# Attention with memory and a gated feed-forward: diagonal score blocks packed at 64 tokens, 18 score visits a segment in place of 20

## Chip, cores and metric

One core of one Trainium2 chip runs the whole program in one launch. The metric is the device time in microseconds. TensorE is called PE, its weight loader PEld, VectorE DVE, ScalarE ACT, GpSimd POOL, and SyncE, which issues nearly all transfers, SP.

## The reference

The input x has 2048 tokens of 640 features. After a layer norm (xn) there are two branches, and the result is `x + s * g`.

- s: attention with 32 heads of 20 features. The tokens are cut into 4 segments of 512. In a segment each head attends causally to the tokens of that segment alone, and also reads a memory made from all segments before.
- g: `silu(down(sigmoid(xn Wgate) * (xn Wup)))`, with 1536 inner features.

```python
logits = jnp.einsum('bhqd,bhkd->bhqk', qs, ks) * scale + mask     # mask: query < key
p = _softmax(logits, axis=-1)
a_dot = jnp.einsum('bhqk,bhkd->bhqd', p, vs)
pq = phi(qs)
num = jnp.einsum('bhld,bhde->bhle', pq, M)
den = jnp.einsum('bhld,bhd->bhl', pq, z)[..., None] + 1e-06
o = g * (num / den) + (1.0 - g) * a_dot
pk = phi(ks)
M = M + jnp.einsum('bhld,bhle->bhde', pk, vs)
z = z + jnp.einsum('bhld->bhd', pk)
```

All data are bfloat16.

## The kernel before

Heads are taken in 8 groups of four. In a group, head r lies in the row strip of 32 partitions from 32r (20 features of the head and 4 rows that carry a bound, 24 in all), so that four score products of four heads run side by side in four row strips of PE. `QT` and `KT` hold the transposed queries and keys of half of the groups; they come through DRAM (`stage_out`, `relay`, `c_out`, `c_in`).

Scores are made transposed: keys on partitions, queries on columns. A *visit* (`scores`, line 628) fills `Sps`, one tile of four PSUM banks, 512 columns for each of the four heads. One exponential on ACT (line 639) takes the whole tile to `pt` in SBUF, of which there are four buffers; `Sps` has one. The causal mask is put on afterwards by POOL with affine selects (line 643), which set the upper part of the diagonal blocks to zero.

Of the 512 x 512 scores of a head, only blocks of 128 keys by the queries from the block on are made: 4 x 128 columns on the diagonal and 768 beside it, 1280 in all. Two groups (a pair) make 2560 columns, five visits of 512. `UNITS` is the table of these five: which group of the pair, which key block, which query blocks, how many, and at which column. Units 0 and 3 hold the four diagonal blocks of a group and are masked with four selects each. A segment has 4 pairs, 20 visits (`NSLOT`), the kernel 80.

`weigh_group` (line 661) multiplies the exponentials of one group by the values: `AT` is 128 x 512, head r on partitions 32r to 32r+31 (column strips of PE), the weights are V with a column of ones beside each head (`VW` = 21), so that row 20 of a strip is the softmax denominator. ACT copies AT to `ats` scaled by the gate's share, an SP transpose makes `Asb`, `divide` on DVE divides, `o_add` adds the memory's part `om`.

All other products are full size: v, k and q of the next segment, gate, up and down, the output product, the memory reads (`am`). The same function `mm` (line 193) can issue each of them as four column strips of 32 output partitions (line 196) in place of one (line 199); it does so in the slots just before an AT (`columns`).

Order: the engines' instructions are written out by hand. A slot is one visit. Python code at build time fills each slot: first AT if one is due, then the visit's scores, then *tasks* (products with a due time in slots, from `PLAN`) and *bulk* (gate, up, down) up to a common level. `PLAN` has due times in slots for every segment: `v`, `k`, `q` products, `pk`/`pq` (phi), `stats`/`norm`, `proj`, `read`, transfers `wd`, `wo`, `xr`, `rows`, and a correction of the bulk for each slot, `bias`. `LAG` has the delays after an AT, in slots. `later` puts something a while after its task. So the order on each engine is fixed; what waits at run time are semaphores.

SP issues transfers and transposes in its own fixed order. The startup (line 707) is written out separately; the main loop begins at the first scores (33.2 us in the profile); after the last AT (297.4 us) the last down products and the output product follow.

Of the kernel before, what the change touches and what calls it, by code (L numbers as in the profile page):

```python
# [9 lines left out]
P = 128  # L10
S = 2048
D = 640
# [41 lines left out]
NU = len(UNITS)  # L54
NSLOT = NG // 2 * NU
# [5 lines left out]
LAG = [0.5, 2.9, 1.9]  # L61
LAST = (NSEG - 1, NG // 2 - 1)
# [4 lines left out]
    dict(glu=[-1.9, -4.08],  # L67
         wd=[4.2, 7.1, 5.93, 5.73],
         wo=[18.5, 20.03],
         v=[1.4, 1.63, 2.65, 3.07, 3.82, 4.8, 5.74, 6.86],  # L70
         k=[5.3, 7.42, 7.86, 8.11, 8.64],
         q=[10.0, 10.58, 11.02, 13.03, 15.22],
         pk=[8.9, 9.37, 10.91, 12.19, 13.55],
         pq=[13.9, 14.48, 15.42, 16.05, 18.25],
         pk0=[0.41, 1.17, 2.49],
         bound=16.1,
         upd=[9.12],
         norm=[-1.9, -0.26],
         late=4.1,
         rows=[11.82, 12.73],  # L80
         bias=[-0.2, -0.3, 0.0, 0.1, 0.0, 0.4, -0.3, 0.5, 0.2, 0.0, 0.4, 0.1, -0.1, -0.1, -0.3, 0.2, 0.4, -0.2, 0.0, -0.3],
         dg=[0, 1, 0, 0]),
    dict(v=[2.8, 3.74, 4.2, 4.5, 4.79, 5.23, 5.54, 6.62],
         k=[6.1, 7.53, 7.69, 8.63, 10.59],
         q=[13.0, 13.26, 13.64, 14.61, 15.74],
         pk=[9.2, 9.5, 11.64, 13.19, 13.89],
         pq=[14.7, 15.49, 15.61, 16.18, 18.08],
         bound=17.0,
         upd=[9.16],
         stats=[-1.9, -1.23, -2.6, -1.59],  # L90
         norm=[-0.2, 0.84, 2.41, 2.85],
         proj=[6.4, 7.01, 7.37, 8.1, 9.14, 10.03, 11.29, 12.57],
         read=[2.2, 2.88, 3.42, 4.8, 5.37, 5.77, 6.53, 6.86],
         turn=[2.6, 2.72, 3.87, 4.97],
         xr=[3.93, 5.14, 5.18, 9.5],
         rows=[10.32, 10.94],
         bias=[-0.8, 0.7, -0.1, -0.1, 0.2, -0.2, -0.2, -0.5, -0.3, 0.0, 0.7, 0.3, 0.0, -0.1, -0.1, 0.1, -0.5, 0.1, -0.1, 0.0],
         dg=[0, 0, 0, 1]),
    dict(v=[2.5, 2.71, 4.39, 4.62, 5.59, 6.19, 6.59, 7.25],
         k=[7.6, 8.6, 8.82, 10.45, 10.63],  # L100
         q=[11.7, 11.92, 12.21, 12.71, 13.01],
         pq=[13.9, 14.67, 17.25, 17.4, 18.21],
         bound=14.3,
         upd=[10.97],
         stats=[-1.9, -0.84, 1.22, 2.68],
         norm=[-0.7, 0.06, 2.22, 4.3],
         proj=[4.7, 4.88, 5.44, 6.41, 8.53, 9.28, 9.51, 9.97],
         read=[2.9, 4.34, 4.71, 5.64, 6.52, 7.12, 7.61, 9.05],
         turn=[3.2, 3.91, 4.6, 5.28],
         xr=[2.53, 3.76, 4.58, 6.49],  # L110
         bias=[0.3, -0.1, 0.6, -1.1, -0.4, -0.5, 0.8, 0.2, 1.2, -0.4, 0.6, 1.3, -0.1, -0.4, -0.2, 0.3, 0.3, -0.3, -0.2, -0.1],
         dg=[0, 1, 1, 1]),
    dict(proj=[5.7, 6.98, 7.43, 8.44, 9.0, 10.74, 11.23, 11.81],
         read=[2.7, 3.67, 5.0, 5.2, 6.87, 7.73, 8.63, 9.25],
         turn=[3.6, 4.03, 5.33, 5.39],
         xr=[3.83, 4.67, 7.15, 9.08],
         xl=[-8.0, -5.88, -5.57, -5.21],
         bias=[0.1, 0.1, 0.1, 0.1, -0.4, 0.0, 0.0, 0.2, 0.1, -0.8, 0.1, 1.0, -0.3, 0.4, -0.5, 0.0, 0.5, 0.0, -0.3, -0.5],
         dg=[0, 1, 0, 1]),
# [4 lines left out]
def kernel(  # L124
# [130 lines left out]
    wt = cpool.tile([P, P], BF, name="wt")  # L255
    nc.vector.memset(wt[:], 0.0)
# [7 lines left out]
    for i in range(8):  # L264
        V.append(cpool.tile([P, H + 1, VW], BF, name=f"va{i}"))
    QT = [cpool.tile([P, 4, L], BF, name=f"QT{i}") for i in range(3)]
    KT = [cpool.tile([P, 4, L], BF, name=f"KT{i}") for i in range(3)]
    nInd = cpool.tile([P, DC, H], F32, name="nInd")
    BD = cpool.tile([P, DC, HW, VW], BF, name="BD")
# [14 lines left out]

    def make_ind():

        nc.gpsimd.memset(nInd[:], -1.0)
        nc.gpsimd.affine_select(out=nInd[:], in_=nInd[:], compare_op=ALU.is_ge, fill=0.0,
                                base=0, pattern=[[P, DC], [-DH, H]], channel_multiplier=1)
        nc.gpsimd.affine_select(out=nInd[:], in_=nInd[:], compare_op=ALU.is_ge, fill=0.0,  # L290
                                base=DH - 1, pattern=[[-P, DC], [DH, H]], channel_multiplier=-1)

    def make_bd(a, b):
        if a == 0:
            nc.gpsimd.memset(BD[:], 1.0)
# [14 lines left out]
    def gates():  # L310
        th = cpool.tile([P, H], F32, name="th")
        nc.scalar.activation(th[:], beta_b[:], ACT.Tanh, scale=0.5)
        gcol = cpool.tile([P, H], F32, name="gcol")
        gin["omg"] = cpool.tile([P, H], F32, name="omg")
        gin["ginv"] = cpool.tile([P, H], F32, name="ginv")
        nc.vector.tensor_scalar(gcol[:], th[:], 0.5, 0.5, op0=ALU.mult, op1=ALU.add)
        nc.vector.tensor_scalar(gin["omg"][:], th[:], -0.5, 0.5, op0=ALU.mult, op1=ALU.add)
        nc.vector.reciprocal(gin["ginv"][:], gcol[:])
# [148 lines left out]
    def v_tile(n, j, half):  # L467
# [6 lines left out]
        evacuate(va[:, half * 16:(half + 1) * 16, 0:DH], ps[:].rearrange("p (h e) -> p h e", e=DH))  # L474

# [19 lines left out]
    def m_update(n):  # L495
# [11 lines left out]
        dmb = stg.tile([P, DC, WIN, VW], BF, name="dmb", bufs=2)  # L507
# [120 lines left out]
    def scores(n, pair, u):  # L628
        half = pair // 2
        qt, kt = half_tile(QT, n, half), half_tile(KT, n, half)  # L630
        for (dg, kb, qb, cnt, c0) in UNITS[u]:
            gi = 2 * pair % 4 + dg
            for r in range(4):
                nc.tensor.matmul(Sps[:, r, c0:c0 + cnt * P],  # L634
                                 lhsT=kt[32 * r:32 * r + KR, gi, kb * P:(kb + 1) * P],
                                 rhs=qt[32 * r:32 * r + KR, gi, qb * P:(qb + cnt) * P],
                                 start=True, stop=True, tile_position=(32 * r, 0))
        pt = ptp.tile([P, 4, L], BF, name="pt")
        nc.scalar.activation(pt[:], Sps[:], ACT.Exp, scale=SCALE)  # L639
        if u in (0, 3):  # L640
            for r in range(4):
                diag = pt[:, r, :].rearrange("p (x c) -> p x c", c=P)
                nc.gpsimd.affine_select(out=diag, in_=diag, compare_op=ALU.is_ge, fill=0.0, base=0,  # L643
                                        pattern=[[0, 4], [1, P]], channel_multiplier=-1)
        return pt

    def parts(dg):
        return [(u, kb, qb, cnt, c0) for u in range(NU) for (d, kb, qb, cnt, c0) in UNITS[u] if d == dg]

# [11 lines left out]
    def weigh_group(now, n, pair, dg, pts):  # L661
        g = 2 * pair + dg
        AT = dtile([P, L], F32, "AT")
        mine = sorted(parts(dg), key=lambda m: m[0] == 3 + PLAN[n]["dg"][pair])
        for i, (u, kb, qb, cnt, c0) in enumerate(mine):
            v = V[4 * (n % 2) + kb][:].rearrange("p h e -> p (h e)")
            for r in range(4):
# [168 lines left out]
    for n in range(NSEG):  # L836
# [46 lines left out]
        for slot in range(NSLOT):  # L883
# [7 lines left out]
            elif u == 3:  # L891
                weigh_group(now, n, pair, 0, pts)
# [60 lines left out]
```

## Time and profile before

Three runs took 317.45, 319.76 and 320.02 us; the median is 319.76. The profiled execution took 317.42 us.

| | profile before |
|---|---|
| time of the profiled execution | 317.42 us |
| its span (first to last instruction) | 315.7 us |
| granted PE clock, mean | 0.999 |
| PE busy | 306.9 us (97%) |
| ACT busy | 250.5 us (79%) |
| DVE busy | 202.5 us (64%) |
| POOL busy | 133.9 us (42%) |
| exponentials (line 639) | 80, 1876 ns each |
| selects (line 643) | 128, 664 ns each |
| DMA engines | 52.4% of the span |

Busy time is the time in which an engine runs at least one instruction; the rest is idle time, and the profile names what ended it. Idle time of an engine that does not set the end costs nothing. A PE product takes some 0.2 us longer from start to end than its columns need, since products overlap; so PE's pace is read from the distance of starts, not from the duration of one.

### The profile page before, as it was taken

What the parts mean: (1) busy time and instruction counts of PE and PEld (TensorE: products, weight loads), DVE (VectorE), ACT (ScalarE), POOL (GpSimd) and SP (SyncE); (2) the same over time, 40 slices, a digit from 0 to 9 for tenths busy, and PEclk for the clock granted to TensorE, in tenths of its full rate; (3) what the DMA queues carried; (4) which work ended last, traced back from release to release, by engine and by line L of the source; (5) the groups of instructions that cost most, each with busy time, mean ns of one, the idle gap of its engine ahead of it and who ended that gap; (6) DMA issues with size and microseconds to landing.
All of it is one profiled execution on the core that took longest, in us unless ns stands there. A gap on an engine that the chain in (4) does not pass through costs nothing.

```text
span 315.7 us, 11686 instructions
## 1 busy us (share of the span) xinstructions
PE 306.9 (97%) x4989; PEld 175.7 (56%) x5021; DVE 202.5 (64%) x472; ACT 250.5 (79%) x284; POOL 133.9 (42%) x248
## 2 busy tenths in 40 slices
PE   7999999999999999999999999999999999999995
PEld 6544555545574566545566565645466655544773
DVE  6476653596885657688767867787554487733345
ACT  7654899999997886797888878887998978889530
POOL 4176424273355230483316543377444333643305
PEclk9999999999999999999999999999999999999999
DMA  7985995957965770645531494245400452330042
GB/s 235 356 267 160 233 175 159 274 151 184 158 137 106 86 139 23 193 99 156 128 104 36 92 129 117 83 142 171 98 20 21 77 126 62 102 77 19 19 69 83
DMA packets 71395, 39.95 MB, mean 127 GB/s; under 512 B 46000, under 2 KB 71344, under 8 KB 71344
## 3 DMA queue, kind: packets, MB, share of 16 engines
q1 hardware_dynamic: 71200, 39.05, 52.4%
q8 instruction: 39, 0.64, 0.9%
q10 hardware_dynamic: 144, 0.16, 0.1%
q14 instruction: 12, 0.10, 0.1%
HBM read 20.19 MB, written 8.39 MB: 91 GB/s over the span
## 4 chain that ended last, share of the span: by engine, by line
PE 96%; DVE 1%; issue 1%; DMA 1%; POOL 0%
PE gp L199 12%; PE up L199 12%; PE yp L199 10%; PE Sps L634 8%; PE yp L196 7%; PE psq L199 6%; PE AT L669 6%; PE psk L199 5%; PE up L196 5%; PE gp L196 5%; PE psv L199 5%; PE sp L199 5%; PE sp L196 2%; PE psv L196 2%; PE psk L196 2%; PE psq L196 1%
## 5 line engine op out<-in xcount | busy, mean ns | idle before, releaser
L639 ACT ACTIVATE pt<-Sps 128x2048 bf16<-128x2048 f32 x80 | 150.1, 1876 | 14.4 <-PE Sps L634 12.8
L643 POOL TENSOR_SCALAR_AFFINE_SELECT pt<-pt 128x512 bf16<-128x512 bf16 x128 | 80.5, 664 | 138.3 <-ACT pt L639 138.2
L554 DVE SCALAR_TENSOR_TENSOR hT<-hT,up 128x512 bf16<-128x512 bf16 x48 | 32.9, 685 | 38.4 <-ACT hT L543 17.8
L199 PE MATMUL gp<-xnT,Wg 128*128 128x512 bf16 x162 | 43.4, 380 | 0.8 <-issue 0.5
L199 PE MATMUL up<-xnT,Wu 128*128 128x512 bf16 x159 | 42.4, 379 | 1.4 <-issue 1.1
L543 ACT ACTIVATE hT<-gp 128x512 bf16<-128x512 f32 x48 | 28.6, 598 | 9.2 <-PE gp L199 8.8
L199 PE MATMUL yp<-Wd,hT 128*128 128x320 bf16 x230 | 34.1, 300 | 0.0
L634 PE MATMUL Sps<-QT,KT 24*128 24x128 bf16 (+2 forms) x896 | 31.9, 241 | 0.0
L573 DVE SCALAR_TENSOR_TENSOR aa<-t,yp 128x320 bf16<-128x320 bf16 x32 | 15.3, 480 | 24.9 <-ACT t L571 24.8
L673 ACT ACTIVATE ats<-AT,share 128x512 bf16<-128x512 f32 x32 | 22.0, 688 | 9.2 <-PE AT L669 8.5
L199 PEld LDWEIGHTS <-hT 128*128 128x128 bf16 x230 | 21.6, 98 | 10.3 <-issue 1.1
L199 PEld LDWEIGHTS <-Wu 128*128 128x128 bf16 x172 | 16.1, 98 | 17.8 <-issue 0.6
L199 PEld LDWEIGHTS <-Wg 128*128 128x128 bf16 x172 | 15.8, 98 | 17.8 <-issue 1.5
L634 PEld LDWEIGHTS <-KT 24*128 24x128 bf16 x896 | 13.1, 92 | 21.7 <-issue 20.5
L669 PE MATMUL AT<-pt,va 128*32 128x128 bf16 (+2 forms) x896 | 23.5, 242 | 0.1
L196 PE MATMUL yp<-Wd,hT 128*32 128x320 bf16 x616 | 22.6, 300 | 0.0
L571 ACT ACTIVATE t<-yp 128x320 bf16<-128x320 f32 x32 | 13.9, 438 | 9.2 <-PE yp L199 6.7
L669 PEld LDWEIGHTS <-va 128*32 128x32 bf16 x896 | 17.8, 97 | 5.8 <-DVE aa L611 0.3
L656 DVE TENSOR_TENSOR od<-Asb,rd 128x320 bf16<-128x320 bf16 x32 | 18.2, 568 | 2.6 <-DVE rd L655 1.6
L611 DVE SCALAR_TENSOR_TENSOR aa<-aa,sp 128x320 bf16<-128x320 bf16 x32 | 15.4, 483 | 6.7 <-PE sp L199 4.4
L199 PE MATMUL psq<-xnT,Wq 128*128 128x512 bf16 x81 | 19.3, 379 | 0.3 <-issue 0.2
L196 PEld LDWEIGHTS <-hT 128*32 128x32 bf16 x616 | 15.7, 97 | 5.5 <-issue 1.5
(97 smaller groups left out, 454.3 us busy)
## 6 DMA issues: line engine op xcount, KB each, us to landing
xt<-in_A_x_dram SPq DMA_DIRECT2D x8, 320.0 KB
KT<-Ks SPq DMA_DIRECT2D x32, 80.0 KB
QT<-Qs SPq DMA_DIRECT2D x32, 80.0 KB
Wg<-in_B_w_gate_dram SPq DMA_DIRECT2D x3, 640.0 KB
Wu<-in_B_w_up_dram SPq DMA_DIRECT2D x3, 640.0 KB
Wd<-in_B_w_down_dram SPq DMA_DIRECT2D x4, 480.0 KB
xr<-in_A_x_dram SPq DMA_DIRECT2D x12, 160.0 KB
out_dram<-xr SPq DMA_DIRECT2D x12, 160.0 KB
```

Source lines behind the costliest of these rows:

```text
L196: nc.tensor.matmul(ps[b:b + 32], lhsT=lhsT[:, b:b + 32], rhs=rhs, start=start, stop=stop, tile_position=(0, b), skip_group_check=True)
L199: nc.tensor.matmul(ps, lhsT=lhsT, rhs=rhs, start=start, stop=stop, skip_group_check=True)
L543: nc.scalar.activation(h[:], gp[:], ACT.Tanh, scale=0.5)
L554: empty(lambda: nc.vector.scalar_tensor_tensor(out=h[:], in0=h[:], scalar=1.0, in1=ps[:], op0=ALU.add, op1=ALU.mult), own)
L573: empty(lambda: nc.vector.scalar_tensor_tensor(out=aa[:, hs], in0=t2[:], scalar=1.0, in1=yp[:], op0=ALU.add, op1=ALU.mult), own)
L611: nc.vector.scalar_tensor_tensor(out=aa[:, hs], in0=aa[:, hs], scalar=0.25, in1=sp[:], op0=ALU.mult, op1=ALU.mult)
L634: nc.tensor.matmul(Sps[:, r, c0:c0 + cnt * P], lhsT=kt[32 * r:32 * r + KR, gi, kb * P:(kb + 1) * P], rhs=qt[32 * r:32 * r + KR, gi, qb * P ...
L639: nc.scalar.activation(pt[:], Sps[:], ACT.Exp, scale=SCALE)
L643: nc.gpsimd.affine_select(out=diag, in_=diag, compare_op=ALU.is_ge, fill=0.0, base=0, pattern=[[0, 4], [1, P]], channel_multiplier=-1)
L656: nc.vector.tensor_tensor(s["od"][:, :, 4 * g * DH:(4 * g + 4) * DH].rearrange("p q (r e) -> p q r e", e=DH), A[:, :, :, 0:DH], rd[:].unsq ...
L669: nc.tensor.matmul(AT[32 * r:32 * r + 32, qb * P:(qb + cnt) * P], lhsT=v[:, h0:h0 + 32], rhs=pts[u][:, r, c0:c0 + cnt * P], start=(i == 0) ...
L673: nc.scalar.activation(ats[:], AT[:], ACT.Identity, scale=gin["share"][:, g:g + 1])
```

## The change

Each 128 x 128 diagonal block is cut at 64. Its right part (the last 64 queries against all 128 keys) joins the columns beside it: kinds 0 to 3, `UPPER`, 448, 320, 192 and 64 columns. Its left part needs only the first 64 keys against the first 64 queries. Two of these small blocks, of two key blocks, are put into the same 64 columns, one on partitions 0 to 63, one on 64 to 127: kinds 4 and 5. A group then has 1024 + 128 = 1152 columns, four groups (a half) 4608, nine visits. `VISITS` is the table: group, kind, column, width. A segment has 18 visits, the kernel 72. Visits 0, 3, 5 and 7 of a half hold packed pieces, and in them every score product is issued with 64 keys as weights, two for each strip, on eight strips (32 rows by 64 columns); in the other visits with 128 keys as before.

For AT, a packed piece is multiplied twice, each time over all 128 partitions: with `VE`, whose lower half is zero, and with `VO`, whose upper half is zero. VE holds the first 64 tokens of V tiles 0 and 2, VO those of tiles 1 and 3, moved 64 partitions down; `v_low` copies them by four SP transfers a segment, `v_zeros` sets the zero halves once, on POOL in the startup.

Masks: in a packed piece two selects on 64 partitions each, in the first part of each kind 0 to 3 one over 64 columns; pieces that stand 256 columns apart are done together. It makes 240 selects for 128.

The AT of groups 0 to 3 of a half stand ahead of its slots 3, 5, 7 and 9 (the ninth is slot 0 of the next half); before, one stood at units 3 and 0 of each pair. All due times in `PLAN` and the delays `LAG` are new. W_down comes in 12 transfers of one tile (160 KB) in place of 4 of three. To make room in SBUF, `wt` and `BD` share a buffer with `om`, `nInd` is bfloat16, `dmb` has one buffer and the gate's small tiles are reused.

```diff
-UNITS = [
-    [(0, kb, kb, 1, kb * P) for kb in range(4)],
-    [(0, 0, 1, 3, 0), (0, 2, 3, 1, 384)],
-    [(0, 1, 2, 2, 0), (1, 1, 2, 2, 256)],
-    [(1, kb, kb, 1, kb * P) for kb in range(4)],
-    [(1, 0, 1, 3, 0), (1, 2, 3, 1, 384)],
+HP = P // 2
+UPPER = [(kb, kb * P + HP, L - kb * P - HP) for kb in range(4)]
+VISITS = [
+    [(0, 4, 0, 64), (0, 5, 64, 64), (0, 3, 128, 64), (0, 0, 192, 320)],
+    [(0, 1, 0, 320), (0, 2, 320, 192)],
+    [(0, 0, 0, 128), (1, 1, 128, 320), (1, 3, 448, 64)],
+    [(1, 4, 0, 64), (1, 0, 64, 192), (1, 5, 256, 64), (1, 2, 320, 192)],
+    [(1, 0, 0, 256), (2, 2, 256, 192), (2, 3, 448, 64)],
+    [(2, 4, 0, 64), (2, 5, 64, 64), (2, 0, 128, 64), (2, 1, 192, 320)],
+    [(2, 0, 0, 384), (3, 0, 384, 128)],
+    [(3, 4, 0, 64), (3, 5, 64, 64), (3, 0, 128, 320), (3, 3, 448, 64)],
+    [(3, 1, 0, 320), (3, 2, 320, 192)],
 ]
...
-NSLOT = NG // 2 * NU
+NSLOT = 2 * NU
+WEIGH = [NU * (g // 4) + (3, 5, 7, 9)[g % 4] for g in range(NG)]
...
-LAG = [0.5, 2.9, 1.9]
+LAG = [0.45, 3.3, 1.7]
...
+    def v_low(n, j):
+        dst = VO[HP:P] if j % 2 else VE[0:HP]
+        nc.sync.dma_start(dst[:, j // 2, :], V[4 * (n % 2) + j][0:HP].rearrange("p h e -> p (h e)")[:, 0:LOWW])
...
-    def scores(n, pair, u):
...
+    def scores(n, half, u):
         qt, kt = half_tile(QT, n, half), half_tile(KT, n, half)
-        for (dg, kb, qb, cnt, c0) in UNITS[u]:
-            gi = 2 * pair % 4 + dg
+        for (gi, kind, c0, w, q0, _) in PIECES[u]:
             for r in range(4):
-                nc.tensor.matmul(Sps[:, r, c0:c0 + cnt * P],
-                                 lhsT=kt[32 * r:32 * r + KR, gi, kb * P:(kb + 1) * P],
-                                 rhs=qt[32 * r:32 * r + KR, gi, qb * P:(qb + cnt) * P],
-                                 start=True, stop=True, tile_position=(32 * r, 0))
+                rows = slice(32 * r, 32 * r + KR)
+                wide = P if all(p[1] < 4 for p in PIECES[u]) else HP
+                for i in range(P // wide):
+                    t0 = kind * P + i * wide if kind < 4 else (2 * (kind - 4) + i) * P
+                    f0 = q0 if kind < 4 else t0
+                    nc.tensor.matmul(Sps[wide * i:wide * i + wide, r, c0:c0 + w], lhsT=kt[rows, gi, t0:t0 + wide],
+                                     rhs=qt[rows, gi, f0:f0 + w], start=True, stop=True,
+                                     tile_position=(32 * r, wide * i), skip_group_check=True)
         pt = ptp.tile([P, 4, L], BF, name="pt")
         nc.scalar.activation(pt[:], Sps[:], ACT.Exp, scale=SCALE)
...
+    def mask(pt, pieces):
+        for gi in sorted({p[0] for p in pieces}):
+            for low in (True, False):
+                cols = [p[2] for p in pieces if p[0] == gi and p[5] and (p[1] >= 4) == low]
+                if len(cols) == 2 and cols[1] - cols[0] == L // 2:
+                    spans = [pt[:].rearrange("p r (x c) -> p (r x) c", c=L // 2)[:, :, cols[0]:cols[0] + HP]]
+                else:
+                    spans = [pt[:, :, c:c + HP] for c in cols]
+                for t in spans:
+                    for rows in ((slice(0, HP), slice(HP, P)) if low else (slice(0, P),)):
+                        nc.gpsimd.affine_select(out=t[rows], in_=t[rows], compare_op=ALU.is_ge, fill=0.0,
+                                                base=0 if low else HP, pattern=[[0, t.shape[1]], [1, HP]],
+                                                channel_multiplier=-1)
...
+        for u, pieces in enumerate(PIECES):
+            for (d, kind, c0, w, qs, _) in pieces:
+                if d != gi:
+                    continue
+                if kind < 4:
+                    runs = [(V[4 * (n % 2) + kind][:].rearrange("p h e -> p (h e)"), qs)]
+                else:
+                    runs = [((VE, VO)[i][:, kind - 4, :], (2 * (kind - 4) + i) * P) for i in range(2)]
+                for v, q0 in runs:
+                    for r in range(4):
+                        h0 = (4 * g + r) * VW
+                        nc.tensor.matmul(AT[32 * r:32 * r + 32, q0:q0 + w], lhsT=v[:, h0:h0 + 32],
+                                         rhs=pts[half, u][:, r, c0:c0 + w],
+                                         start=first, stop=True, tile_position=(0, 32 * r), skip_group_check=True)
+                    first = False
...
-    for i in range(4):
-        at(PLAN[0]["wd"][i], 0, load_late, "d", B_w_down, 3 * i, 3 * i + 3)
+    for i in range(FC):
+        at(PLAN[0]["wd"][i], 0, load_late, "d", B_w_down, i, i + 1)
```

More of the change, by code (lines that the diff above doesn't have):

```diff
@@ L83 @@
[L83 to L98, printed above, removed]
@@ L474, in v_tile @@
         evacuate(va[:, half * 16:(half + 1) * 16, 0:DH], ps[:].rearrange("p (h e) -> p h e", e=DH))
+        if half == 1:
+            if n == 0 and j == 3:
+                later(0.4, v_low, n, j)
     def phi(n, src, c):
@@ L638, in scores @@
         pt = ptp.tile([P, 4, L], BF, name="pt")
         nc.scalar.activation(pt[:], Sps[:], ACT.Exp, scale=SCALE)
[L640 to L644, printed above, removed]
-        return pt
-    def parts(dg):
-        return [(u, kb, qb, cnt, c0) for u in range(NU) for (d, kb, qb, cnt, c0) in UNITS[u] if d == dg]
+        mask(pt, PIECES[u])
@@ L758, in startup @@
         v_ones(4, 8)
+        v_zeros()
+        for j in range(3):
+            v_low(0, j)
         take(2)
@@ L883 @@
         for slot in range(NSLOT):
[L884 removed]
+            half, u = divmod(slot, NU)
             now = NSLOT * n + slot
             share = max(level - fixed[slot], 0.0)
[L887 to L894 removed]
+            if now in TURNS:
+                weigh_group(now, *TURNS[now], pts)
+            pts[half, u] = scores(n, half, u)
+            columns[0] = now + 1 in TURNS
             delay[0] = True
```

167 lines of the change are left out of this document (91 added, 76 removed).

## The prediction

> **What bounds the kernel now.** I read the engine table first, then the waits, then the order of time, then the groups of one shape. The profiled execution took 317.42 us around a span of 315.7 us. Three timed runs gave 317.45, 319.76 and 320.02 us, so the profile is one of the quick ones, 2.3 us (0.7%) below the median. I add my difference to the median. About 1% (3.2 us) is what a measurement of this kernel can tell from no change.
>
> ```profile
> PE 306.9 (97%) x4989; PEld 175.7 (56%) x5021; DVE 202.5 (64%) x472; ACT 250.5 (79%) x284; POOL 133.9 (42%) x248
> ```
>
> ```profile
> POOL pt L643 <- ACT pt L639: 138.2, 31, 9.6
> ...
> PEld L634 <- issue: 20.5, 68, 0.4
> ...
> ACT pt L639 <- PE Sps L634: 12.8, 26, 0.9
> ...
> PE wps L705 <- DVE wt L256: 1.0, 1, 1.0
> ```
>
> PE is busy 97% of the span, and PE is hardly ever in the waits as the one that waits: one microsecond at the start, nothing for ACT or POOL in the loop. ACT waits for PE, POOL waits for ACT. So the time is the length of PE's own list, plus startup and ending. ACT's 250.5 us would matter only if PE stood waiting for an exponential. The loader's 20.5 us ahead of the scores is no wait for anybody's data; the order of time shows what it is:
>
> ```profile
> 101.74 0.59 PE L199 MATMUL gp<-xnT,Wg 128*128 128x512 bf16 x2
> ...
> 102.27 0.40 PE L634 MATMUL Sps<-QT,KT 24*128 24x256 bf16 x8
> ...
> 102.60 0.83 PE L196 MATMUL gp<-xnT,Wg 128*32 128x512 bf16 x12
> 102.78 1.88 ACT L639 ACTIVATE pt<-Sps 128x2048 bf16<-128x2048 f32 x1 [0.94 <-PE Sps L634]
> ...
> 105.34 0.73 PE L669 MATMUL AT<-pt,va 128*32 128x128 bf16 x28
> ...
> 106.00 0.40 PE L634 MATMUL Sps<-QT,KT 24*128 24x128 bf16 x16
> ...
> 106.34 0.34 PE L199 MATMUL am<-Mbd,q 128*128 128x147 bf16 x3
> ```
>
> ```profile
> 107.75 1.08 PE up L199 x5
> ```
>
> The chain that ended last gives the rate: five products of 512 columns in 1.08 us, 0.216 us for 512 columns, 0.42 ns a column. A visit's scores are 512 columns for each of four row strips that run side by side, so 0.216 us; but from the scores at 106.00 to the next product at 106.34 it is 0.34 us, 0.12 more. Before them, 1280 columns of AT should take 0.54 us and take 0.66, 0.12 more. The other visit here reads 0.53-0.43 = 0.10 and 0.33-0.216 = 0.11. PE loses about 0.11 us whenever the shape of its tiles changes (full to row strips, row strips to column strips, and back). A visit costs 0.216 + 2x0.11 = 0.44 us.
>
> **The change, part by part.**
>
> *Eight fewer visits (20 to 18 a segment, four segments).* PE: 8 x 0.44 = -3.5 us, half columns, half changes of shape (the built order has 150 such changes where there were 166). ACT loses 8 exponentials of 1.876 us, 15 us; PE does not wait for ACT, so this is worth nothing. The other products of PE keep their columns. More of the bulk stands in slots that use column strips (the built order has 65 products more cut in four); that costs nothing, since 154 sets of the cut yp products (616 records) take 22.6 us, 147 ns each, and 230 uncut ones 34.1 us, 148 ns each.
>
> ```profile
> L199 PE MATMUL yp<-Wd,hT 128*128 128x320 bf16 x230 | 34.1, 300 | 0.0
> ...
> L196 PE MATMUL yp<-Wd,hT 128*32 128x320 bf16 x616 | 22.6, 300 | 0.0
> ```
>
> *AT.* The columns stay 1280 a group, because each packed diagonal piece is streamed twice, once for VE and once for VO. There are 9 sets of four products where there were 7: 64 sets more, 168 of them 64 wide. The nearest row is dm, 63 columns wide in the same column strips:
>
> ```profile
> L503 PE MATMUL dm<-va,pkt x240: 190/197/205, 62.2 to 208.0; 128*32 128x63 bf16 x120
> ```
>
> In its starts one by one, the first sets of four follow each other at 29 ns and the later ones at 33.5; the columns alone would be 26.3. So the extra is 64 x 2.5 ns = 0.2 us at least and 168 x 7 ns = 1.2 us at most. AT comes behind long bulk products, while the queue is full, so I take 0.3.
>
> *Scores of the packed visits (32 of 72).* Every product there is 24 rows by 64 columns of weights, eight strips at once, 32 products a visit instead of 8 or 16. No row shows this shape. The columns streamed are the same 512 if all eight run side by side. Low bound: as dm's first sets, nothing to add. Next: eight starts at dm's later pace of 8.4 ns make 67 ns for a set of 64 columns instead of 27; 11 such sets in a half, 88 in all, x 40 ns = 3.5 us. High bound: the two column halves of a strip do not overlap, and all 32 x 512 columns are streamed twice, +6.9 us. AT stands just ahead in 31 of the 32 and lets the queue fill, which is nearer the low end; I take 1.5. The changes into and out of this shape are not in the trace either: between as cheap as the others and one load more (0.03 us) each, 0 to 1.0 each way (32 each); I take 0.4.
>
> [...]
>
> *Masks.* 240 selects replace 128. Width 168 takes 393 ns and width 512 takes 664, so one of width 256 costs between them; by the straight line 0.46 us. 216 x 0.46 + 24 x 0.66 = 115 us against 128 x 0.66 = 85. POOL goes to about 52%. That is covered by the slots between a visit and its AT, except in one place: the last visit of a half now has both masked pieces of group 3, and AT reads them at the very next slot. Exponential starts 0.51 after the scores (102.27 to 102.78), takes 1.88, two masks 0.92: ready 3.4 us after the scores began. In the built order PE has 3.25 to 4.5 us of columns from these scores to the next ones (seven of the eight places), plus 0.2 for changes of shape, and reaches the masked columns about 0.2 before the end. In the tightest three the two are within 0.15 us of each other. I take 0.3 us in all; if the cover goes, see the rivals.
>
> *Transfers.* Sixteen copies of half a V tile and eight more Wd issues: 24 more on SP, 0.4 us each (as `Wd` at 52.67). The first four copies and the Wd pieces fall between 33 and 62 us, 12 x 0.4 = 5 us more on a queue that issues nearly back to back there. What is late next is the Asb transposes, whose result divide needs only 3.3 slots (12 us) later, and the stage-out of k for segment 1 (60.35 us before), needed a half segment later. Wd itself is first read at 75.5 us; the same bytes land by then. Copies in later segments wait for group 7's AT, as the transposes ahead of them do already. 0 on PE; if the cover goes, 1 to 3 us once. Two memsets of 1366 columns on POOL (840 take 0.80 us, so 1.3 each) end before the first mask.
>
> *The slot table* keeps about the same due times in microseconds (old numbers x 3.3 us a slot, new x 3.6). Nothing priced; the waits it may bring are in the range.
>
> Sum: -3.5 + 0.3 + 1.5 + 0.4 + 0.3 = -1.0; 0.2 for waits I cannot place gives -0.8. On the profile's 317.42 that is 316.6, on the median 319.0 us.
>
> **The rivals.**
> 1. *The small sets are free.* Sets run at 29 ns and changes cost as before: -3.5 + 0.2 = -3.3, 316.4 us. For it: dm's first sets; starts 4 ns apart inside a set. Against it: the eight-strip shape is unseen, and it needs every wait to be nothing. This is also the floor, since PE has nothing more to give back.
> 2. *Eight strips do not overlap* (the slower end). The 16,384 columns stream twice: -3.5+0.3+6.9+0.4+0.3 = +4.4, 324.2 us. It decides once more than some 3 us of the 6.9 appear. Against it: column strips overlap in AT, and row strips in the scores, each fully; for it: no row has both.
> 3. *The last mask of a half is late.* If the exponential stands behind one evacuation on ACT (0.43 to 0.69 us), or the masks behind one `od` addition on POOL (0.81), AT waits some 0.6 us at most turns from one half to the next, 8 x 0.6 = 4.8, where I have 0.3: +3.7, 323.5 us. From 0.4 us a place this already passes the middle. For it: seven tight places; against: PE waited for no mask before, and a wait of one slot leaves later slots with slack.
>
> **How the numbers follow.** Forecast (no change that can be told) 0.50; rival 1 0.24; rival 2 0.13; rival 3 0.13. The likeliest is 319.0, its own range 316.8 to 321.5. The range to 315.6 below takes rival 1 with the spread of the median, and to 324.4 above it takes rivals 2 and 3 at their prices. Faster by over 1%: 0.24 (rival 1); slower: 0.26 (rivals 2 and 3); within: 0.50.
>
> **What would show it.** Right: PE still the engine without waits; exponentials 72; from a packed visit's first product to the next other product 0.35 to 0.45 us; AT to the scores after it 0.65 to 0.72. Wrong: that stretch over 0.5 us (rival 2), idle PE or AT waiting for POOL at the first slot of a half (rival 3), PE waiting for a transfer of VE, VO, Wd or KT, or a startup of other length before the first scores (33.2 us now).

## The result, and the profile after

The changed kernel takes 323.04 us (median of six runs, 322.21 to 324.05), the kernel before beside it 318.9 us (317.38 to 320.28). The ratio is 1.0132, 95% interval 1.0088 to 1.0175: slower by 1.3%, 4.1 us. The profiled execution took 322.21 us around a span of 320.5 us, at a granted clock of 0.999 as before. So the span is 4.8 us longer than before's, and this is what has to be explained.

From the profile's page of the kernel after, the engine table, the first line of the chain that ended last, and two groups (busy, mean ns of one, then the idle time before them and what ended it; the first group's mean is over selects of four shapes):

```profile
PE 306.5 (96%) x5952; PEld 177.8 (55%) x5984; DVE 202.7 (63%) x478; ACT 234.8 (73%) x270; POOL 160.8 (50%) x354
...
PE 84%; DVE 6%; DMA 4%; issue 2%; POOL 2%; SPq 1%; ACT 0%; DVEq 0%; ACTq 0%
...
L684 POOL TENSOR_SCALAR_AFFINE_SELECT pt<-pt 128x256 bf16<-128x256 bf16 (+3 forms) x232 | 104.0, 458 | 119.9 <-ACT pt L670 112.6
L670 ACT ACTIVATE pt<-Sps 128x2048 bf16<-128x2048 f32 x72 | 135.0, 1875 | 20.6 <-PE Sps L666 14.8
```

PE is busy for 0.4 us less than before, in a span that is longer: PE now waits. The chain says the same. Before, 96% of it was PE's:

```profile
PE 96%; DVE 1%; issue 1%; DMA 1%; POOL 0%
```

Now it is 84%, and DVE, transfers and POOL stand in it.

Where it waits is seen in a table by stretches. The columns are the length, then busy time of PE, PEld, DVE, ACT and POOL, clock, DMA share and GB/s. First before, then after:

```profile
60.00:100.00 40.00, 39.58 (x747) 22.39 (x749) 31.42 (x74) 37.46 (x44) 21.83 (x37) 1.00 0.78 159
...
200.00:297.00 97.00, 95.68 (x1740) 53.38 (x1753) 56.86 (x129) 83.44 (x82) 45.94 (x70) 1.00 0.32 80
```

```profile
60.00:100.00 40.00, 36.09 (x878) 21.26 (x881) 27.72 (x70) 32.14 (x39) 20.88 (x46) 1.00 0.71 165
...
200.00:297.00 97.00, 95.68 (x2093) 53.43 (x2099) 60.61 (x135) 78.23 (x78) 52.51 (x106) 1.00 0.39 88
```

Between 60 and 100 us PE loses 3.5 us of busy time; in the last 97 us, where the same share of the visits is of the new kind, nothing. The new shapes as such do not cost it; something in the first segment does. The waits of after, longest kinds left out:

```profile
POOL rstd L372 <- DVE mv L368: 7.2, 4, 3.4
...
DVE k L512 <- DMA Ks<-k: 4.4, 1, 4.4
...
DVE q L512 <- DMA Qs<-q: 2.6, 1, 2.6
...
PE gp L215 <- DVE q L457: 1.6, 1, 1.6
...
PEld L215 <- DMA xnT<-xn: 1.3, 1, 1.3
...
PE AT L714 <- POOL pt L684: 1.0, 1, 1.0
```

Of these six only POOL's wait for `mv` has a counterpart before (9.4 us, with no AT behind it). They are two chains and a late transpose. The first, in order of time:

```profile
65.27 0.91 SPq L445 DMA_DIRECT2D Ks<-k  x2
...
69.69 0.36 DVE L512 TENSOR_SCALAR k<-k 128x512 bf16<-128x512 bf16 x1 [4.36 <-DMA Ks<-k]
70.50 0.68 DVE L457 CAST q<-psq 128x512 bf16<-128x512 f32 x1
71.24 1.24 PE L215 MATMUL gp<-xnT,Wg 128*128 128x512 bf16 x5 [1.64 <-DVE q L457]
```

phi works in place: its first operation on DVE (line 512) overwrites the k tile that the transfer to `Ks` is still reading. That transfer is issued at 65.27 us, behind Wd pieces on SP; in the kernel before it was issued some 5 us earlier, and phi there began at 64.63 us, 4.3 us behind the issue, without a wait:

```profile
60.35 1.82 SPq L419 DMA_DIRECT2D Ks<-k  x2
```

In the kernel after, phi is let go only at 69.69 us, 4.4 us behind the issue. DVE stands for 4.36 us with everything queued behind phi, among it the evacuation of q (line 457), and PE has no free PSUM tile for gp: 1.7 us.

The second, 27 us later, on POOL and then PE:

```profile
93.99 0.22 POOL L372 TENSOR_SCALAR rstd<-mv 128x1 f32<-128x1 f32 x1 [3.38 <-DVE mv L368]
94.29 0.65 POOL L373 TENSOR_TENSOR rstd<-rstd,nhalf 128x1 f32<-128x1 f32 x1
94.91 2.31 POOL L684 TENSOR_SCALAR_AFFINE_SELECT pt<-pt 64x256 bf16<-64x256 bf16 x5
```

```profile
98.04 0.86 POOL L684 TENSOR_SCALAR_AFFINE_SELECT pt<-pt 128x256 bf16<-128x256 bf16 x2
98.51 0.71 PE L714 MATMUL AT<-pt,va 128*32 128x320 bf16 x8 [1.01 <-POOL pt L684]
99.15 0.44 PE L666 MATMUL Sps<-QT,KT 24*64 24x64 bf16 x32
99.52 1.25 PE L215 MATMUL gp<-xnT,Wg 128*128 128x512 bf16 x4
```

Again phi in place, now of q, waits for the transfer that reads q (2.6 us); behind it on DVE stand the means of the next layer norm, POOL waits for them (3.4 us) with the masks queued behind, and AT of the last group of the half waits for the masks, 1.5 us in two pieces (a first piece of 0.2 us is not counted).

Besides these, PE pauses in the middle of a set of short products, with no data to wait for ("issue"):

```profile
136.89 0.23 PE L666 MATMUL Sps<-QT,KT 24*64 24x64 bf16 x7
...
137.75 0.41 PE L666 MATMUL Sps<-QT,KT 24*64 24x64 bf16 x25 [0.63 <-issue]
```

Adding up the distances of PE's starts, every pause over 0.12 us beyond the columns and a change of shape counts as a wait; the sums are good to some 0.2 us. In the loop they come to 0.25 us before and 7.2 us after: 0.6 at 54 us (v's product, `psv`; its evacuation stands behind k's, which waits for the last transpose of `pkt`), 0.6 at 64 (a pause without data), 1.7 at 71, 0.4 at 77, 0.3 at 87, 1.5 at 98, 0.8 at 138 (no data), 1.3 at 198 (`xnT`; the addition that makes `om` on DVE ends there within 0.1 us of it). Pauses in the startup are 0.6 us shorter. What is left up to the start of PE's last product, PE's own list, is 309.2 us before and 307.7 after, 1.5 shorter. 6.9 - 0.6 - 1.5 = 4.8 us, the difference of the spans.

### The profile page after: what moved, and what is told of

Read it like the earlier page. It is cut to its first block, busy times and chain, and to the rows that moved or that the text cites. A ratio compares the mean times of both kernels' runs of the same rounds, so it can differ in the third digit from the quotient of the medians.

```text
span 320.5 us, 13754 instructions
## 1 busy us (share of the span) xinstructions
PE 306.5 (96%) x5952; PEld 177.8 (55%) x5984; DVE 202.7 (63%) x478; ACT 234.8 (73%) x270; POOL 160.8 (50%) x354
## 4 chain that ended last, share of the span: by engine, by line
PE 84%; DVE 6%; DMA 4%; issue 2%; POOL 2%; SPq 1%; ACT 0%; DVEq 0%; ACTq 0%
PE gp L215 11%; PE up L215 9%; PE yp L215 8%; PE Sps L666 7%; PE yp L212 6%; PE up L212 5%; PE AT L714 5%; PE sp L215 4%; PE psk L215 4%; PE psv L215 4%; PE psq L215 4%; PE gp L212 4%; PE sp L212 3%; PE psv L212 2%; PE psk L212 2%
## 5 line engine op out<-in xcount | busy, mean ns | idle before, releaser
L684 POOL TENSOR_SCALAR_AFFINE_SELECT pt<-pt 128x256 bf16<-128x256 bf16 (+3 forms) x232 | 104.0, 458 | 119.9 <-ACT pt L670 112.6
L670 ACT ACTIVATE pt<-Sps 128x2048 bf16<-128x2048 f32 x72 | 135.0, 1875 | 20.6 <-PE Sps L666 14.8
L215 PE MATMUL up<-xnT,Wu 128*128 128x512 bf16 x143 | 38.0, 380 | 1.1 <-issue 0.8
L719 ACT ACTIVATE ats<-AT,share 128x512 bf16<-128x512 f32 x32 | 22.0, 687 | 13.6 <-PE AT L714 11.5
L215 PE MATMUL yp<-Wd,hT 128*128 128x320 bf16 x210 | 31.2, 300 | 0.0
L666 PE MATMUL Sps<-QT,KT 24*64 24x64 bf16 (+8 forms) x1408 | 30.1, 231 | 1.0 <-issue 0.6
L666 PEld LDWEIGHTS <-KT 24*64 24x64 bf16 (+1 forms) x1408 | 13.6, 102 | 22.2 <-issue 20.7
L212 PE MATMUL yp<-Wd,hT 128*32 128x320 bf16 x696 | 25.8, 300 | 0.0
L714 PE MATMUL AT<-pt,va 128*32 128x320 bf16 (+5 forms) x640 | 23.1, 252 | 1.2 <-POOL pt L684 1.0
L212 PE MATMUL up<-xnT,Wu 128*32 128x512 bf16 x348 | 23.1, 381 | 0.0
L609 POOL TENSOR_TENSOR od<-od,om 128x320 bf16<-128x320 bf16 x20 | 16.5, 831 | 5.2 <-DVE od L694 5.2
```

The costliest lines, as they stand in the source:

```text
L212: nc.tensor.matmul(ps[b:b + 32], lhsT=lhsT[:, b:b + 32], rhs=rhs, start=start, stop=stop, tile_position=(0, b), skip_group_check=True)
L215: nc.tensor.matmul(ps, lhsT=lhsT, rhs=rhs, start=start, stop=stop, skip_group_check=True)
L609: eng.tensor_tensor(o, o, st[n]["om"][:, :, cs], op=ALU.add)
L666: nc.tensor.matmul(Sps[wide * i:wide * i + wide, r, c0:c0 + w], lhsT=kt[rows, gi, t0:t0 + wide], rhs=qt[rows, gi, f0:f0 + w], start=True, ...
L684: nc.gpsimd.affine_select(out=t[rows], in_=t[rows], compare_op=ALU.is_ge, fill=0.0, base=0 if low else HP, pattern=[[0, t.shape[1]], [1, HP]],
L714: nc.tensor.matmul(AT[32 * r:32 * r + 32, q0:q0 + w], lhsT=v[:, h0:h0 + 32], rhs=pts[half, u][:, r, c0:c0 + w], start=first, stop=True, ti ...
```

## The experiments

Ratios are to the kernel before, run beside each. The theory: PE's list got shorter as forecast, and waits ate more than that. What is to be found is whether one part of the change makes the waits.

**Wd in four transfers again, in the changed kernel.**

```diff
-wd=[4.0, 4.15, 4.5, 4.55, 5.2, 5.75, 5.4, 6.55, 6.9, 7.25, 7.6, 7.95]
+wd=[4.0, 4.55, 5.4, 7.25]
...
+    for i in range(4):
+        at(PLAN[0]["wd"][i], 0, load_late, "d", B_w_down, 3 * i, 3 * i + 3)
```

> The changed kernel with W_down again in 4 transfers of three tiles, at the due times 4.0, 4.55, 5.4 and 7.25; all else as changed. Theory A (SP is late: 12 issues of about 0.5 us each, among relays and transposes, push the stage-out of segment 1's keys from 60.4 to 65.3 us, DVE's phi waits 4.4 us for that transfer to have read the keys, the query evacuations queued behind it come late, and PE stands 1.6 us at 71 us): DVE's wait for Ks falls below 1 us, the PE stall at 71 us goes, ratio to the kernel before 1.006 to 1.010 instead of 1.013. Rival B (the bytes, not the issues, are late; the transfer engines are shared): nothing moves, 1.013. Rival C (the table of due times as a whole is what is late): the stall moves but the sum stays at 1.011 to 1.013.

Measured: 1.0159 [1.0101, 1.0218]. `Ks` was issued at 61.07 us, and PE's wait at 71 us was gone, as were those at 54, 77 and 87 us and all but 0.2 us of that at 98. The worth did not appear: a pause without data, 0.6 us in the changed kernel, took 3.7 us.

```profile
67.33 0.19 PE L714 MATMUL AT<-pt,VE 128*32 128x64 bf16 x1 [3.55 <-issue]
```

While PE stands there, the engines behind it catch up (phi still waited 2.4 us for `Ks`), so it is not shown that four transfers by themselves cure the waits after 67 us. Three of the four runs had a mean clock of 0.989 to 0.994, where the six of the changed kernel had 0.998 to 1.0; the last section comes back to this.

**No copies of V**: `VE` and `VO` are filled with ones and never copied, so the packed pieces are multiplied with other values.

```diff
-        nc.gpsimd.memset(VE[HP:P], 0.0)
-        nc.gpsimd.memset(VO[0:HP], 0.0)
+        nc.gpsimd.memset(VE[:], 1.0)
+        nc.gpsimd.memset(VO[:], 1.0)
...
     def v_low(n, j):
+        return
```

> The changed kernel without the 16 copies of half V tiles: VE and VO are set to one once, so the packed diagonal pieces are multiplied with wrong values; instructions on PE, ACT and DVE are the same. Theory A (SP is late in segment 0: the four copies and the transfers between them take SP 3.3 us from 33 to 40 us, the last pkt transpose goes out at 48.8 instead of 46.4 us and DVE's evacuation of the next keys, which reuses that buffer, holds PE for 0.4 to 0.6 us at 54 us): the stall at 54 us goes and the one at 71 us shrinks by up to 1 us; 1.008 to 1.011. Rival B (copies are covered): 1.013, both stalls as they were.

Measured: 1.0104 [1.0062, 1.0146]. The wait at 54 us is gone, and so are those at 77 and 87 us and nearly all of that at 98; the one at 70 us stays with 2.0 us (`Ks` issued at 65.62). The time is 0.9 us below the changed kernel's, which is inside the intervals, so what sixteen copies are worth is not told by the times.

**Wd in twelve transfers in the kernel before** (the twelve due times times 20/18, since its slots are shorter).

> The kernel before with one part of the change alone: W_down in 12 transfers, at the changed kernel's due times put into slots of the kernel before (times 20/18). Theory A (issues on SP count): the keys of segment 1 go out 2 to 4 us later than 60.4 us, DVE waits for them, PE stalls 0.5 to 2 us between 60 and 75 us; ratio 1.002 to 1.006. Rival B (bytes count, not issues): 0.999 to 1.001.

Measured: 0.9994 [0.9965, 1.0024]. `Ks` was issued at 62.83 us, 2.5 us later than in the kernel before, and phi, which is due later in this order, waited only 0.6 us for it. With room in the order twelve transfers cost nothing that can be told.

**The changed kernel with the due times of before**, times 18/20, its lags likewise, and Wd in four; the corrections of the bulk and the times of the copies stay the change's.

```diff
-LAG = [0.45, 3.3, 1.7]
+LAG = [0.45, 2.61, 1.71]
...
-         k=[5.07, 6.88, 7.37, 7.6, 8.08],
+         k=[4.77, 6.68, 7.07, 7.3, 7.78],
...
```

> The changed kernel (18 visits, packed pieces, copies) with the due times of the kernel before times 18/20, its delays after AT scaled the same, and W_down in 4 transfers; the correction of the bulk by slot and the due times of the copies stay those of the change. Theory A (the packed visits themselves are a gain of 2 to 3 us on PE, and what costs is the order of SP and DVE that the new table makes): the stalls between 54 and 99 us go, PE's list is shorter than before by 1.7 us of columns and about 1.8 us of changes of shape, ratio 0.990 to 1.000. Rival D (the packed visits and the 240 masks cost it whatever the table): stalls at masks and scores remain in other places, 1.008 to 1.015.

Measured: 1.0336 [1.0281, 1.0392], 329.37 us, with 11.5 us of waits in the loop. The largest:

```profile
PE AT L714 <- DMA VO<-va: 4.0, 1, 4.0
```

A copy of V comes too late for the first AT there. So the new table is not the cause as such; it is better than the old one. The visits need an order of their own.

**phi later** in the first segment's part of the table:

```diff
-         pk=[8.11, 9.19, 9.67, 9.95, 11.56],
-         pq=[12.61, 13.1, 13.61, 14.35, 15.06],
+         pk=[9.3, 9.4, 9.7, 10.0, 11.56],
+         pq=[12.61, 13.1, 13.61, 15.2, 15.6],
```

> The changed kernel with DVE's phi of segment 1's first keys and last queries due later (keys 9.3, 9.4, 9.7, 10.0 in place of 8.11, 9.19, 9.67, 9.95; last two query chunks 15.2, 15.6 in place of 14.35, 15.06); no transfer is moved. Theory A2 (a phi in place waits in DVE's fixed order until the transfer of the same buffer has read it; all that stands behind it on DVE, the evacuations of PSUM and the sums that POOL's list waits for, comes late, and PE with it at 71, 77, 87 and 98 us): DVE's waits for Ks and Qs fall below 0.5 us each, the four stalls (3.8 us together) go to under 1; ratio 1.002 to 1.006. Rival F (PE would have run into the next wait there anyhow: instructions, buffers): the stalls come back elsewhere, 1.010 to 1.014.

Measured: 1.0063 [1.0024, 1.0102]. The waits at 54, 71, 77 and 87 us are gone, and the time falls by about 2 us (the two intervals just overlap). That is the most direct test of the first chain: only phi moved. The second is not cured: phi of q still waits 1.8 us for `Qs`, and near 96 us PE waits 2.0 us where it waited 1.5 at 98, 0.6 of them because the scores now wait for the bound rows (`QT<-Cs`).

**The memory update earlier** (80 short `dm` products with their 80 loads, in front of both pauses without data):

```diff
-         upd=[8.01],
+         upd=[7.3],
...
-         upd=[8.04],
+         upd=[7.3],
```

> The changed kernel with the memory update (160 short PE instructions in 0.8 us) of the first two segments at slot 7.3 in place of 8.0, so that whole products of 512 columns follow it and not quartered products, an AT of 36 and packed scores of 32 products. [...]

Measured: 1.0118 [1.0073, 1.0163]. The two pauses are gone from where they were, but two shorter ones (0.3 and 0.5 us) now stand among the `dm` products themselves. And the five additions to `Mbd` on POOL, 3.5 us together, now stand in front of masks, and AT waits 2.4 us in three places:

```profile
62.97 3.49 POOL L542 TENSOR_TENSOR Mbd<-Mbd,dmb 32x315 bf16<-32x315 bf16 x5
66.53 0.85 POOL L684 TENSOR_SCALAR_AFFINE_SELECT pt<-pt 128x256 bf16<-128x256 bf16 x2
```

**Both, and two more times** (two v products of the third segment at 6.7 and 6.9, the first k product of the second at 5.7).

> Both edits together, and two more of the same kind: the last two value products of segment 3 at 6.7 and 6.9 in place of 5.83 and 6.03 (PE stood 1.3 us at 198 us for the transpose of xn), and the first key product of segment 1 at 5.7 in place of 5.07 (0.57 us at 54 us for the buffer of the old keys). If the waits are all that costs (A2 and I), PE's list alone is left: 8 visits fewer for 3.5 us, 64-wide sets of weights about 1 us, so 314.5 to 317.5 us, ratio 0.990 to 0.998. If waits only move (rival F): 1.004 to 1.012.

Measured: 1.0089 [1.0057, 1.0122]; 3.7 us of waits in the loop. The late `xnT` at 198 us is cured, the `Mbd` additions cost 1.4 us at 66, and a pause among the `dm` products 0.7 us at 129.

**Only the packed pieces 64 wide**, their neighbours in the same visit 128 wide:

```diff
-                wide = P if all(p[1] < 4 for p in PIECES[u]) else HP
+                wide = P if kind < 4 else HP
```

> The changed kernel with only the packed pieces 64 columns of weights wide; the other pieces of the packed visits are 128 wide as before (256 score products fewer, 48 more changes of shape). If a change of width alone costs PE what a change between strips and full size does, 0.1 us: +4 to +5 us less 0.5 for wide sets, ratio 1.023 to 1.030. If it costs nothing, and 64-wide sets cost 23 ns each: -0.5 us, 1.010 to 1.014.

Measured: 1.0242 [1.0204, 1.028], as the first reading, a change of width that costs 0.1 us, wanted. 256 score products fewer, but 48 more changes of width, and PE's list is 312.7 us, 5.0 more than the changed kernel's: about 0.1 us for a change of column width alone. Keeping all products of a visit at 64 columns is the better choice.

**The update later** (10.3 in both places, where full-size products follow):

```diff
-         upd=[8.01],
+         upd=[10.3],
...
-         upd=[8.04],
+         upd=[10.3],
```

> The changed kernel, with the memory update of the first two segments (upd: 160 dense dm products and what follows them) a little over two slots later (10.3 for 8.01 and 8.04), where full-size products follow it and no AT. [...]

Measured: 1.0111 [1.0068, 1.0154]. No pause at either place is left in its profile (which has a clock of 0.949, so its other waits are not compared). That fits short products ahead of the pauses as what makes them, and speaks against data of the update. Of the 1.4 us of the two pauses at most 0.7 is seen in the time, and that is inside the intervals.

**phi later, update later, v later, and the third Wup load behind the first copies** (`glu=[1.19, 0.9]`).

> The changed kernel with only due times moved: phi as in the run with phi later, the update of the first two segments at 10.3, two v products of the third segment 0.7 to 0.9 slots later, the third load of Wup after the copies of V instead of ahead of them. Theory A (the 4.8 us by which the changed kernel's span is longer are waits that the new table made, each at its own place, and PE's own list is really about 2 us shorter): 314.5 to 317.5 us, ratio 0.990 to 1.000, with PE idle in the loop under 2.5 us. Rival B (waits taken from one place come back at another, since the engines behind PE have no slack left in this order): ratio 1.003 to 1.010, with 4 us or more of idle PE in the loop, at new places.

Measured: 1.0048 [1.0024, 1.0071], 320.43 us, the best of all versions. It is better than the change by 0.8% and still worse than before. Waits in the loop are 4.2 us, most of them at new places: k's evacuation behind `pkt` (1.1), a phi in front of `hT` (0.9), the bound rows (1.0), masks behind `Mbd` (0.7).

**Without masks and phi, on both sides.** POOL and DVE lose most of what PE waited for; k and q stay as they are and no mask is put on.

```diff
-        ex = stg.tile([P, L], BF, name="ex", tag="ex", bufs=3)
-        nc.scalar.activation(ex[:], t, ACT.Exp)
...
-            nc.vector.tensor_scalar(t, t, 1.0, 1.0, op0=ALU.add, op1=ALU.max)
-            nc.vector.tensor_tensor(t, ex[:], t, op=ALU.min)
...
-        mask(pt, PIECES[u])
```

The kernel before in this form:

> The kernel before without its masks and without phi: no selects on POOL (85 us of its busy time) and none of phi's exponentials and vector operations, so that k and q stay as they are and the result is another. PE's list is the same. Both theories: PE waited only 0.25 us in the loop, so 0.996 to 1.001 of the kernel before, 317.6 to 319.3 us.

The changed kernel in this form:

> The changed kernel, without masks and phi in the same way. It takes away what POOL and DVE make PE wait for at 71, 77, 87 and 98 us, and probably the late xnT at 198; the two instruction gaps (1.4 us) may stay. Theory A (PE's own list is about 2 us shorter than before, the rest is waits): 316.0 to 319.0 us, ratio to the kernel before 0.991 to 1.000, and 0 to 2 us below the other kernel of this pair. Rival B (the list itself is no shorter, small products cost more than the starts show): 320 us or more, ratio 1.004 or more, 2 us above the other of the pair, with PE idle in the loop under 2 us.

Measured: 320.44 us, 1.0013 [0.998, 1.0047], and 323.57 us, 1.0109 [1.0062, 1.0157]. The changed one is still 3.1 us behind, so the time is in rival B's range, but not for rival B's reason: PE's list is 309.2 us at a clock of 0.997 on one side and 309.7 at 0.994 on the other, that is 308.3 and 307.9 at full clock. The waits of the loop are 3.0 and 6.1 us; 1.9 of the 3.0 are one wait for the transposed `oT`, which the kernel before does not have. With POOL and DVE mostly free, PE of the changed kernel waits for transfers, or, in the second line, at a place where its loader waits 1.3 us for the late `xnT`:

```profile
PE Sps L662 <- DMA QT<-Cs: 1.4, 3, 1.0
PE psv L215 <- DVE om L554: 1.1, 1, 1.1
...
PE up L215 <- DMA Wu<-in_B_w_up_dram: 0.4, 1, 0.4
PE AT L709 <- DMA VO<-va: 0.4, 1, 0.4
```

All these transfers come from SP's queue, and the bound rows show how late it is: `Cs` was sent at 85.46 us in the kernel before and at 90.50 in the changed one, 5 us later. Before, the first scores that read them began at 94.49 us, 3.5 us after the last issue of `QT<-Cs` ended (90.97). In the changed kernel it ended at 96.25 and the scores began at 99.15, 2.9 us later, and 1.5 of these are the wait for the masks. In the best version, where cured waits bring PE there sooner, the scores began at 97.19, 0.4 us after the last issue, and then waited.

**Two more rounds of due times.** The first starts from the best version: k 0.7 slots later, one phi 0.4 later, the last q product and the bound 0.4 and 0.3 earlier, the third segment's update 0.4 earlier.

> The run before this one with due times alone (1.0048), with five more times moved: the first k product of the second segment 0.7 slots later, one phi 0.4 later, the last q product and the bound of that segment 0.4 and 0.3 earlier, the memory update of the third segment 0.4 earlier. Theory A (each of its five waits, 4.2 us together, stands for a due time): 316.5 to 319 us, ratio 0.992 to 1.001. Rival (waits come back elsewhere): 1.002 to 1.008.

Measured: 1.0167 [1.0118, 1.0215]. The scores wait 2.9 us for `QT<-Cs`, and four of the six runs have a mean clock of 0.989. The second moves the last q products and the bound 0.6 to 0.8 earlier, three phi 0.4 to 0.6 and the first k product 0.4 later:

```diff
...
-         q=[9.0, 9.72, 9.92, 12.53, 13.7],
-         pk=[9.3, 9.4, 9.7, 10.0, 11.56],
+         q=[9.0, 9.72, 9.92, 11.9, 12.9],
+         pk=[9.3, 9.4, 10.3, 10.6, 12.0],
...
-         bound=14.49,
+         bound=13.7,
```

> The run at 1.0048 with the last two q products of the second segment 0.6 and 0.8 slots earlier and the bound 0.8 earlier (so that the bound's transfers are issued some 3 us earlier), three phi 0.4 to 0.6 later, the first k product 0.4 later. Theory A (the order has room, each wait goes with its due time; PE's own list, times the clock, is 1.0 to 1.5 us shorter than before): waits of PE in the loop under 2 us, 315.5 to 318.5 us, ratio 0.990 to 1.000. Rival (DVE and SP have no room left around 55 to 100 us, a wait taken away comes back): 3.5 us or more of waits in the loop, ratio 1.002 to 1.010.

Measured: 1.0205 [1.0163, 1.0247]. The bound now comes before the last phi of q, and its tile shares three buffers with phi's exponentials. So an exponential on ACT has to wait until the transfer has read the bound, and the scores behind it wait for ACT. From ACT's and PE's order of time:

```profile
93.43 0.63 ACT L509 ACTIVATE ex<-q 128x512 bf16<-128x512 bf16 x1 [4.20 <-DMA Cs<-cb]
```

```profile
96.45 0.61 PE L666 MATMUL Sps<-QT,KT 24*128 24x320 bf16 x8 [3.75 <-ACT pt L670]
```

## Why the prediction was wrong

The forecast was 319.0 us, no change that can be told; 323.04 lies inside the range and outside the likeliest case's own range. Its steps, in its order:

- *Eight fewer visits, -3.5*: right to some 0.5 us. PE's columns fell by 1.7 us, and the 150 changes of shape cost 16.0 us where the 166 cost 17.3 (from the last set's start to the next shape's, less the set's columns), together -3.0.
- *AT, +0.3*: right; a 64-wide set costs 2.4 ns over its columns, and all AT sets together 0.65 us over theirs, for 0.51 before.
- *Scores of the packed visits, +1.5*: close. Of 80 measured sets of eight with 64 columns, 32 are followed by the next after 51 to 54 ns and 47 after 28 to 33, where the columns need 27; with the wider sets it is 1.1 us over the columns. The first set of a visit has the longer distance in 31 of the 32 visits, so an AT just ahead did not bring it to the low bound; that a queue fills there was the author's guess. Eight strips do run side by side (starts 3 ns apart), so rival 2 fell.
- *Changes into this shape, +0.4*: into it they cost 0.106 us, like the others; out of it to full products 0.120, where a visit of 128-wide products has 0.104. That is 0.5 us in all, and it is in the 16.0 us above.
- These four made -1.3; PE's list measured -1.5 (307.7 for 309.2), and in the pair without masks and phi -0.4 at full clock. This half of the sum stands.
- *Masks, +0.3*: a select of width 256 takes 0.42 to 0.44 us (0.46 was forecast), and there are 232 selects, 208 of them of this width, where the texts above have 240: 104 us of POOL's time, forecast 115. (The sum of the time until a mask is ready, 0.51, 1.88 and 0.92, makes 3.3 us, not 3.4.) Of the eight tight places one failed, at 98 us, by 1.5 us, and not in the way of rival 3: POOL stood behind layer norm roots that waited for DVE, not behind an `od` addition.
- ***Transfers, 0 on PE***: this step failed. It named the right transfer, the stage-out of k for segment 1, and the wrong one who waits for it. It asked when the data are read next (half a segment later), not when the buffer that the transfer reads is written next: by phi, at 69.69 us, 4 us behind the issue. Late transfers, read like this, are the waits at 54, 71 and 98 us, 3.8 us together, where the text had "1 to 3 us once".
- ***The slot table, nothing priced*, and 0.2 for waits that I cannot place**: this step failed too. The late `xnT` (1.3 us), two short waits (0.7) and two pauses without data (1.4) belong here.

So the mechanism of the gain was right and its size nearly so; the assumption that the engines behind PE keep up was wrong by 6 to 7 us. That a phi in place makes PE wait is shown for the first chain by the run that moved phi alone; the second chain is read from the trace. No part of the change makes the waits by itself: Wd's twelve transfers cost nothing in the old order; without them, or without the copies, several waits go, but one stays or grows, and the time hardly moves; the old due times are worse. Moving due times won back at most 0.8% (1.0048), and each further round opened another wait. Whether some table lets the changed kernel win stays open; its list leaves 0.4 to 1.5 us to win at most. One combination that the traces suggest was not run: Wd in four transfers with the update later, which took the pause without data away.

## What to carry to other kernels

Before an engine that is busy for 97% of the span is given less to do, ask for each transfer on the common queue by how much it slips and who next *writes* the buffer that it reads, not only who reads what it brings: operations in place and shared buffers can turn a transfer that lands in good time into a stall of a whole engine (here 4.4 us on DVE, and 1.7 us on PE behind it). A saving of 0.5% in a list that was fitted to its waits by hand is worth less than the fit; price the loss of the fit, here about 7 us. And a cured wait counts only when the time falls, since the next wait behind it may be the same chain's.

## What the runs showed of the hardware

PE pauses at places where it waits for no data that the profile shows. The changed kernel has two such pauses over 0.5 us in its loop, both in a set of short products: 0.6 us up to 64.31 us and 0.8 us up to 137.75. They end 2.3 and 2.6 us after a packet of 16 KB started on the instruction queue (at 61.97 and 135.17 us). Of these packets there are 47, and 39 before; from the third part of the profile's page after:

```profile
q8 instruction: 47, 0.77, 1.0%
```

PE's recorded products and loads are 11,936, and 10,010 before. In the 3.5 us before the pause at 64 us PE takes 287 of them, 82 a microsecond; in the last third of the loop the mean is 43. The kernel before has a pause of 0.3 us at 133.6 us, in a set of AT. Idle time of PE of 0.5 us or more that ended with "issue" is also in the traces of the first two experiments (3.5 and 0.6 us in the one, 0.5 in the other), of the run with phi later (0.5), of that with both edits (0.5, among the `dm` products), and of the pair without masks and phi (0.7 for the kernel before, 0.9 for the changed one). With the update earlier the pauses are shorter and stand among the `dm` products; with the update later neither of the two is left. So the pauses go with many short products ahead of them; that the packets have to do with them is not shown, nor what ends them.

PE's pace fell in some runs after a wait. In the run without copies, five products of 512 columns take 1.16 us up to the next start, 0.23 us each, and the five after them 2.13 us, 0.43 us each:

```profile
70.22 1.37 PE L215 MATMUL gp<-xnT,Wg 128*128 128x512 bf16 x5 [1.93 <-DVE q L456]
...
71.38 2.34 PE L215 MATMUL up<-xnT,Wu 128*128 128x512 bf16 x5
...
73.51 1.06 PE L215 MATMUL gp<-xnT,Wg 128*128 128x512 bf16 x2
```

In the last round the eight scores behind the wait of 3.75 us take 0.61 us, where eight of these widths take 0.40 in the changed kernel. The mean granted clock is 0.995 in the profiled executions of these two runs, of the old due times and of the round before the last, 0.994 in that of the changed kernel without masks and phi, and 0.999 in the changed kernel's. It does not fall with every wait: in the changed kernel it is 1.00 in each microsecond from 70 to 75 us, where the wait of 1.7 us ends at 71.24, and in the first experiment's profile, with the pause of 3.7 us, it is 0.999. What lowers it is not shown. All six runs of the changed kernel without masks and phi have 0.993 to 0.995 (mean 0.994), the twelve of its counterpart 0.995 to 1.0 (mean 0.999), so an estimated 1.5 us of the 3.1 by which it is behind is this; and the last two rounds, at 0.988 to 0.995 in all runs but one, lose by their waits and once more by the clock.
